# Token mixing's output sums: three float32r products per block, or one plain float32 product

## The chip, the cores and the metric

The kernel runs on one core of one Trainium2 chip. The metric is the time of one execution in device microseconds. The engines are called as the profile calls them: PE is the matrix engine (TensorE) and PEld its loads of stationary operands, DVE the vector engine, ACT the scalar engine, POOL GpSimd, SP the engine that issues most transfers. A matrix product has a stationary operand, which is loaded into the 128x128 array, and a moving operand, whose columns stream past it; the sums stand in PSUM.

## The reference

A decayed linear attention over 4 batches, 8 heads, 768 positions and head size 64, then a mixer of two parts. The attention's output is x, 4 x 768 x 512. Cut to what matters:

```
intra = (qb @ kb.T * Dmask) @ vb             # blocks of 64 positions in the reference
inter = (qb * lam_pow) @ kv_state
xt = x.transpose(0, 2, 1)                    # 4 x 512 x 768
h  = relu(xt @ w_tok1) @ w_tok2              # 768 -> 256 -> 768, over positions
u  = x + h.transpose(0, 2, 1)
h2 = relu(u @ w_ch1) @ w_ch2                 # 512 -> 1536 -> 512, over channels
out = u + h2
```

All inputs are float32 but the four weights of the mixer, which arrive as 64-bit words and are brought to float32 in the kernel. The change concerns the product with w_tok2, called w2 here.

## The kernel before, in words

**Stages.** The first stage, to about 180 us, runs the attention over 16 steps (4 batches, 4 pairs of heads each) and, mixed into it, token mixing. The second, from there to the end, is channel mixing and the output. uT[b] holds u transposed, 512 channels by 768 positions: the attention writes it (`outputs`), token mixing adds to it, channel mixing reads it.

**Token mixing.** For a batch, `token_hidden` (L442) makes the hidden layer: four calls of 128 hidden units by 256 channels, each a sum over six blocks of positions. Every operand stands in two float32r parts, high and low, and a product is three products (high by high, low by high, high by low), so a call is 18 matmuls (L459) of 256 columns. ACT then writes the rectified sum as the high part hh (L463), and DVE the low part hl (L464). `token_out` (L486) and `token_out_pair` (L469, used for the last batch) make the output: a block of 128 channels by 384 positions is a sum over two blocks of hidden units, again in three products each, so 6 matmuls of 384 columns (L496, L479). DVE adds the block to uT (L501, L484). There are 4 batches x 2 halves of positions x 4 blocks of channels = 32 blocks, so 192 matmuls.

**w2.** Its 64-bit words are loaded into the place of uT[2]. In three thirds (`w2_steps`, L432) five steps (`narrow`, L387) bring the words to float32 with scratch in the place of uT[3]: one on ACT (L392) and four on DVE (L393, L396, L399, L402). Then `split` (L383) writes the high part w2h on ACT (L384) and the low part w2l on POOL (L385).

**Plain float32 elsewhere.** The attention's own products use plain float32 operands: scores `sc` (L314: 64 rows of the array, the two heads of a pair in its upper and lower half), outputs `xT` (L333, L343: 64 columns of the array, the two heads left and right) and states `kv` (L270: 64 columns, 64 moving columns). Transposes through PE (L220, L241, L365) take a plain float32 block against an identity over the whole array.

**What sets the order.** The order on every engine is the order in which the program is written. In a step of the attention, scores of the next pair come first, then outputs, states, and between them pieces of token mixing from the list `groups` (as many per step as `take` says). Small steps for ACT, DVE and POOL, those of w2 among them, stand in a queue `waiting`, from which `later(n)` takes one to three at fixed places. Blocks of PSUM come from a ring (`sh`), so a block of output sums can wait until DVE has read an earlier one. `hidp` holds w2h, w2l, the hidden parts hh0, hl0 and h1; channel mixing uses the same places later.

Of the kernel before, what the change touches and what calls it, by code (L numbers as in the profile page):

```python
# [9 lines left out]
F32 = mybir.dt.float32  # L10
F32R = mybir.dt.float32r
AF = mybir.ActivationFunctionType
ALU = mybir.AluOpType
U32 = mybir.dt.uint32
# [8 lines left out]
def kernel(  # L23
# [23 lines left out]
    nc = tc.nc  # L47
    B, H, S, D = q.shape
    DM = H * D
    FT = w_tok1.shape[1]  # L50
    FC = w_ch1.shape[1]
    P = 128
# [3 lines left out]
    NK = FT // P  # L56
    NJ = FC // P
    SB = S // 2
# [5 lines left out]
    waiting = deque()  # L64
# [17 lines left out]
    def bank(tag, nm, n):  # L82
        if tag == "sh" and spare:
            tag = spare.pop()
        return ps.tile([P, n], F32, tag=tag, bufs={"xT": 1, "sh": 3}[tag], name=nm)

    def two_banks(nm, n):
        t = ps.tile([P, 2, 512], F32, tag="sc", bufs=2, name=nm)
        return t[:, :, 0:n]

    hidp = ctx.enter_context(tc.tile_pool(name="hidp", bufs=1, side="right"))
# [107 lines left out]
    n = 1  # L199
    while n < P:  # L200
        nc.vector.tensor_mul(
            out=lamp[:, :, n : 2 * n], in0=lamp[:, :, 0:n], in1=lamp[:, :, n - 1 : n].broadcast_to([P, NP, n])
        )
        n *= 2
    for p in range(NP):
        nc.gpsimd.tensor_copy(
            out=keep[:, p, :, 1:], in_=lamp[:, p, P - 1 : P, None].broadcast_to([P, D, NC - 2])
# [146 lines left out]
    def turn_back(i, g):  # L354
# [21 lines left out]

    w1h = tokp.tile([P, NC, FT], F32R, name="w1h")
    w1l = tokp.tile([P, NC, FT], F32R, name="w1l")
    w2h, w2l = (
        hidp.tile([P, NK, S], F32R, tag=t, name=t) for t in ("w2h", "w2l")  # L380
    )

    def split(hi, lo, src):  # L383
        nc.scalar.copy(out=hi, in_=src)  # L384
        nc.gpsimd.tensor_sub(out=lo, in0=src, in1=hi.bitcast(F32))  # L385

    def narrow(raw, a, sg):  # L387

        low, high = raw[..., 0], raw[..., 1]
        af = a.bitcast(F32)  # L390
        return [
            lambda: nc.scalar.activation(af, high.bitcast(F32), AF.Abs, scale=HIGH_SCALE),  # L392
            lambda: nc.vector.tensor_scalar(  # L393
                out=sg, in0=high, scalar1=0x80000000, scalar2=None, op0=ALU.bitwise_and
            ),
            lambda: nc.vector.scalar_tensor_tensor(  # L396
                out=sg, in0=low, scalar=29, in1=sg, op0=ALU.logical_shift_right, op1=ALU.bitwise_or
            ),
            lambda: nc.vector.tensor_scalar(  # L399
                out=af, in0=af, scalar1=HIGH_MIN * HIGH_SCALE, scalar2=HIGH_MAX * HIGH_SCALE, op0=ALU.max, op1=ALU.min  # L400
            ),
            lambda: nc.vector.scalar_tensor_tensor(  # L402
                out=a, in0=a, scalar=3, in1=sg, op0=ALU.logical_shift_left, op1=ALU.bitwise_or
            ),
        ]

    def words(b):
        return uT[b].rearrange("p t s -> p (t s)").bitcast(U32)
# [22 lines left out]

    def w2_steps(i):  # L432
        n = NK * S // 3
        tmp = words(3)[:, 2 * (i % 2) * n : 2 * (i % 2 + 1) * n]
        a, sg = (x.rearrange("p (k s) -> p k s", k=NK) for x in (tmp[:, :n], tmp[:, n:]))
        ss = slice(i * S // 3, (i + 1) * S // 3)
        raw = words(2).rearrange("p (k s two) -> p k s two", k=NK, two=2)[:, :, ss]
        return narrow(raw, a, sg) + [lambda: split(w2h[:, :, ss], w2l[:, :, ss], a.bitcast(F32))]

    hid = {}  # L440

    def token_hidden(b, half, kk):  # L442

        if half == 0 and kk == 0:
            if b % 2:
                both = hidp.tile([P, 2, NK, DM], F32R, tag="h1", name=f"h{b}")
                hid[b] = both[:, 0], both[:, 1]
            else:
                hid[b] = [hidp.tile([P, NK, DM], F32R, tag=f"{t}0", name=f"{t}{b}") for t in ("hh", "hl")]
        hh, hl = hid[b]  # L450
        xh, xl = x_of[b, half]
        cs = slice(half * DM // 2, (half + 1) * DM // 2)

        ph = bank("sh", f"ph{b}{half}{kk}", DM // 2)
        fs = slice(kk * P, (kk + 1) * P)
        i = 0
        for c in range(NC):
            for w, x in ((w1h, xh), (w1l, xh), (w1h, xl)):
                nc.tensor.matmul(  # L459
                    out=ph, lhsT=w[:, c, fs], rhs=x[:, c], start=(i == 0), stop=(i == 3 * NC - 1)  # L460
                )
                i += 1
        nc.scalar.activation(hh[:, kk, cs], ph, AF.Relu)  # L463
        nc.vector.scalar_tensor_tensor(  # L464
            out=hl[:, kk, cs], in0=ph, scalar=0.0, in1=hh[:, kk, cs].bitcast(F32), op0=ALU.max, op1=ALU.subtract
        )


    def token_out_pair(b, sh, ct):  # L469

        hh, hl = hid[b]
        pu = two_banks(f"pu{b}{ct}{sh}", SB)
        ss = slice(sh * SB, (sh + 1) * SB)
        for y in range(2):
            cs = slice((ct + y) * P, (ct + y + 1) * P)
            i = 0
            for kk in range(NK):
                for h, w in ((hh, w2h), (hl, w2h), (hh, w2l)):
                    nc.tensor.matmul(  # L479
                        out=pu[:, y], lhsT=h[:, kk, cs], rhs=w[:, kk, ss], start=(i == 0), stop=(i == 3 * NK - 1)  # L480
                    )
                    i += 1
        u = uT[b][:, ct : ct + 2, ss]
        nc.vector.tensor_add(out=u, in0=pu, in1=u)  # L484

    def token_out(b, sh, ct):  # L486

        hh, hl = hid[b]

        pu = bank("sh", f"pu{b}{ct}{sh}", SB)  # L490
        cs = slice(ct * P, (ct + 1) * P)
        ss = slice(sh * SB, (sh + 1) * SB)
        i = 0
        for kk in range(NK):
            for h, w in ((hh, w2h), (hl, w2h), (hh, w2l)):
                nc.tensor.matmul(  # L496
                    out=pu, lhsT=h[:, kk, cs], rhs=w[:, kk, ss], start=(i == 0), stop=(i == 3 * NK - 1)
                )
                i += 1
        u = uT[b][:, ct, ss]  # L500
        nc.vector.tensor_add(out=u, in0=pu, in1=u)  # L501

# [37 lines left out]
    def narrow_piece(raw, a, sg):  # L540
        return narrow(raw.rearrange("p (n two) -> p n two", two=2), a, sg)
# [91 lines left out]


    hidden = [[lambda b=b, x=x: token_hidden(b, x // NK, x % NK) for x in range(2 * NK)] for b in range(B)]
    outs = [[lambda b=b, x=x: token_out(b, x // 4, x % 4) for x in range(8)] for b in range(B)]
    groups = deque(hidden[0] + hidden[1][:NK] + outs[0] + hidden[1][NK:] + outs[1])
    for b in range(2, B):
# [6 lines left out]
    idle = [lambda: None]  # L645
# [7 lines left out]
    for i in range(-2, NI):  # L653
# [31 lines left out]
        n = early.get(i, len(work) // 4)  # L685
# [32 lines left out]
        if i == 4:  # L718
            steps = [w2_steps(n) for n in range(3)]
            waiting.extend(2 * idle + steps[0][:5] + idle + steps[0][5:] + steps[1][:2] + idle)  # L720
        if i == 5:
            waiting.extend(steps[1][2:5] + idle + steps[2][:2] + idle + steps[1][5:] + steps[2][2:] + idle)
        if i == 6:
            waiting.append(lambda: load_piece(0, 1, w3[:, 1024:2048]))
            steps = narrow_piece(w3[:, 2048:3072], w3[:, 0:512], w3[:, 512:1024])
            waiting.extend(idle + steps[:1] + 2 * idle + steps[1:2] + 2 * idle + steps[2:])
        if i == 7:
            steps = narrow_piece(w3[:, 1024:2048], w3[:, 512:1024], w3[:, 2048:2560])
# [37 lines left out]
    cs = [cp.tile([P, n * DM], U32, tag=f"cs{x}", name=f"cs{x}") for x, n in enumerate((2, 2, 1))]  # L766
# [12 lines left out]
    steps = {}  # L779
# [7 lines left out]
    for n, fs in enumerate(order):  # L787
        token_out_pair(B - 1, n // 2, 2 * (n % 2))
        for f in fs:
            f()  # L790
# [573 lines left out]
```

## Time and profile before

| | |
|---|---|
| time, median of 2 runs | 553.31 us (553.27 to 553.35) |
| the profiled execution's span | 551.6 us |
| instructions in its trace | 10805 |
| PE busy | 540.1 us of the span (98%), 4180 matmuls |
| DVE, POOL, ACT busy | 438.3, 282.0, 247.6 us |
| granted PE clock, mean | 0.999 of full speed |

The profile is of one execution; its span runs from its first to its last instruction. That execution has no separate time beside its span; the two timed runs lie 1.7 us above it, which is what lies around the span. A PE row's duration is the time of one matmul from its start to the modelled arrival of its last sum; matmuls are pipelined, so what one costs the engine is the distance from its start to the next one's start, not its duration. Busy time counts the durations where they overlap once.

### The profile page before, as it was taken

The numbers are of one execution on the slowest core, as the hardware profiler recorded it, in microseconds if no ns is written. First come the engines' busy times: TensorE is split into PE (matmuls) and PEld (weight loads), VectorE is DVE, ScalarE is ACT, GpSimd is POOL, SyncE is SP. The second block draws the span as 40 slices with busy tenths as digits, with TensorE's granted clock in tenths as the row PEclk, the third lists the DMA queues.
The fourth block names the chain that finished last, engine by engine and source line by source line (L and its number), as shares of the span: only waits on it lengthen the run. The fifth ranks groups of instructions, "written<-read, shape, count | busy, mean of one in ns | idle before, by whom it ended". The sixth has DMA issues, their size and how long they took to land.

```text
span 551.6 us, 10805 instructions
## 1 busy us (share of the span) xinstructions
PE 540.1 (98%) x4180; PEld 527.1 (96%) x4180; DVE 438.3 (79%) x657; ACT 247.6 (45%) x499; POOL 282.0 (51%) x256
## 2 busy tenths in 40 slices
PE   5999999999999999999999999999999999999997
PEld 4889998999999999999999999999999999999996
DVE  4787799687786989887878788788778878779894
ACT  3464543344253454444444443453354555445431
POOL 6667552756213564543444453354475656568450
PEclk9999999999999999999999999999999999999999
DMA  9999999999103523351615300024766132220186
GB/s 185 252 209 193 222 172 182 197 197 157 32 2 114 198 91 118 124 197 43 252 70 203 121 1 1 0 30 65 169 115 198 58 116 58 95 97 2 22 156 130
DMA packets 175683, 66.77 MB, mean 121 GB/s; under 512 B 163600, under 2 KB 165904, under 8 KB 175632
## 3 DMA queue, kind: packets, MB, share of 16 engines
q1 hardware_dynamic: 170400, 64.90, 49.2%
q10 hardware_dynamic: 5232, 1.18, 1.0%
q8 instruction: 33, 0.54, 0.4%
q14 instruction: 18, 0.15, 0.1%
HBM read 49.29 MB, written 16.78 MB: 120 GB/s over the span
## 4 chain that ended last, share of the span: by engine, by line
PE 92%; DMA 3%; DVE 2%; SPq 1%; issue 0%; ACT 0%; ACTq 0%; DVEq 0%
PE po L1043 22%; PE pa L817 13%; PE pc L817 9%; PE pb L817 7%; PE pa L1017 7%; PE ph L459 6%; PE pc L1017 5%; DMA qn<-in_q_dram 3%; PE sc L314 3%; PE pu L496 3%; PE xT L333 3%; PE pd L817 3%; PE xT L343 2%; PE xp L365 2%; PE pu L479 2%; PE kv L270 1%
## 5 line engine op out<-in xcount | busy, mean ns | idle before, releaser
L1056 DVE TENSOR_TENSOR uT<-po,uT 128x768 f32<-128x768 f32 x57 | 54.2, 952 | 16.7 <-PE po L1043 16.4
L832 ACT ACTIVATE c<-c 128x384 f32<-128x384 f32 x42 | 22.1, 526 | 59.2 <-DVE c L877 33.5
L291 POOL COPY stb<-sv 64x320 f32<-64x320 f32 x32 | 26.9, 840 | 38.8 <-DVE sv L278 37.9
L1023 DVE TENSOR_TENSOR uT<-pa,uT 128x768 f32<-128x768 f32 x36 | 34.3, 953 | 9.4 <-PE pa L1017 8.6
L350 ACT COPY uT<-xT 128x384 f32<-128x384 f32 x32 | 15.3, 479 | 46.8 <-PE xT L343 46.7
L834 POOL TENSOR_TENSOR h22l<-c,h22h 128x384 fp32r<-128x384 f32 x14 | 14.4, 1032 | 41.5 <-ACT h22h L833 41.5
L333 PE MATMUL xT<-a,vn 128*64 128x128 f32 x384 | 35.7, 277 | 0.0
L1023 DVE TENSOR_TENSOR uT<-pc,uT 128x768 f32<-128x768 f32 x27 | 25.8, 954 | 11.1 <-PE pc L1017 11.1
L298 DVE TENSOR_TENSOR a<-sc,mask 128x768 f32<-128x768 f32 x32 | 29.1, 947 | 4.6 <-PE sc L314 4.5
L343 PE MATMUL xT<-qs,stb 128*64 128x128 f32 x320 | 31.3, 273 | 0.0
L385 POOL TENSOR_TENSOR c1l<-cs,c1h 128x512 fp32r<-128x512 f32 x15 | 19.3, 1297 | 22.9 <-ACT c1h L384 22.9
L1043 PE MATMUL po<-h12h,c 128*128 128x384 f32 x112 | 28.7, 337 | 0.0
L1043 PE MATMUL po<-h11h,c 128*128 128x384 f32 x112 | 28.6, 336 | 0.0
L1043 PE MATMUL po<-h22h,c 128*128 128x384 f32 x112 | 28.6, 336 | 0.0
L1043 PE MATMUL po<-h21h,c 128*128 128x384 f32 x112 | 28.6, 336 | 0.0
L459 PE MATMUL ph<-xhi,w1h 128*128 128x256 f32 x96 | 28.1, 293 | 0.1
L459 PE MATMUL ph<-xhi,w1l 128*128 128x256 f32 x96 | 27.1, 282 | 0.0
L459 PE MATMUL ph<-xlo,w1h 128*128 128x256 f32 x96 | 27.1, 282 | 0.0
L314 PE MATMUL sc<-qT,kT 64*128 64x128 f32 x384 | 25.8, 281 | 0.3 <-ACT qT L242 0.2
L314 PEld LDWEIGHTS sc<-qT,kT 64*128 64x128 f32 x384 | 22.8, 188 | 3.5 <-issue 2.0
L374 DVE TENSOR_TENSOR xlo<-xp,xhi 128x384 fp32r<-128x384 f32 x32 | 17.7, 552 | 10.3 <-ACT xhi L373 10.0
L257 POOL TENSOR_TENSOR qs<-qT,lamp 128x640 f32<-128x640 f32 x16 | 25.5, 1594 | 0.2
(397 smaller groups left out, 1945.0 us busy)
## 6 DMA issues: line engine op xcount, KB each, us to landing
raw<-in_moe_w_ch_dram SPq DMA_DIRECT2D x20, 512.0 KB, 3.8
vn<-in_v_dram SPq DMA_DIRECT2D x16, 384.0 KB, 5.3
kn<-in_k_dram SPq DMA_DIRECT2D x30, 192.0 KB, 5.2
out_dram<-y SPq DMA_DIRECT2D x104, 48.0 KB, 1.9
qn<-in_q_dram SPq DMA_DIRECT2D x44, 96.0 KB, 3.9
kr<-in_k_dram SPq DMA_DIRECT2D x32, 96.0 KB, 2.7
dc1h<-c1h SPq DMA_DIRECT2D x4, 768.0 KB, 5.4
dc1l<-c1l SPq DMA_DIRECT2D x4, 768.0 KB, 6.7
```

The lines of the kernel that those rows point to most:

```text
L257: nc.gpsimd.tensor_mul(out=qss[i], in0=qTs[i][:, P:].rearrange("p (c i) -> p c i", i=P), in1=lamp[:, p, None, :].broadcast_to([P, NC - 1, P]),
L291: nc.gpsimd.tensor_copy(out=st[r, :, h, :], in_=sv[r].rearrange("p (e c) -> p c e", c=NC - 1))
L298: nc.vector.tensor_mul(out=a, in0=pair.rearrange("p h (c i) -> p h c i", i=P), in1=mask[:, 2 * p : 2 * p + 2, None, :].broadcast_to([P, 2, ...
L314: nc.tensor.matmul(out=sc[h][:, c * P : (c + 1) * P], lhsT=kTs[i][r, cs], rhs=qTs[i][r, cs], start=True, stop=True,)
L333: nc.tensor.matmul(out=xT[h * D : (h + 1) * D, cs], lhsT=vns[i][:, h, c, :], rhs=weights_of[i, g, h][:, cg, :], start=(cg == 0), stop=False,)
L343: nc.tensor.matmul(out=xT[h * D : (h + 1) * D, cs], lhsT=st[:, c - 1, h, :], rhs=qss[i][:, c - 1, :], start=False, stop=(cg == 2),)
L459: nc.tensor.matmul(out=ph, lhsT=w[:, c, fs], rhs=x[:, c], start=(i == 0), stop=(i == 3 * NC - 1))
L817: nc.tensor.matmul(out=to, lhsT=w[:, t], rhs=x[:, t], start=(start and i == 0), stop=(i == 5), skip_group_check=not start,)
L1017: nc.tensor.matmul(out=pair[x][:, t], lhsT=w[:, t], rhs=h, start=(start and i == 0), stop=(i == 2), skip_group_check=not start,)
L1023: nc.vector.tensor_add(out=ub, in0=pair[x], in1=ub)
L1043: nc.tensor.matmul(out=to, lhsT=w[:, jj, t * P : (t + 1) * P], rhs=h, start=(i == 0), stop=(i == 3 * JG - 1))
L1056: nc.vector.tensor_add(out=ub, in0=po, in1=ub)
```

## The change

Token mixing's output sums use plain float32 operands. The hidden layer is written once by ACT, without a low part; w2 is one float32 tile, which the narrowing steps write in place, without a split. Per block of 128 channels by 384 positions there are two products in the program's text in place of six. The hidden sums over w1 and all of channel mixing stay in three products.

```
--- before.py
+++ after.py
@@ -376,9 +376,7 @@
 
     w1h = tokp.tile([P, NC, FT], F32R, name="w1h")
     w1l = tokp.tile([P, NC, FT], F32R, name="w1l")
-    w2h, w2l = (
-        hidp.tile([P, NK, S], F32R, tag=t, name=t) for t in ("w2h", "w2l")
-    )
+    w2 = hidp.tile([P, NK, S], F32, tag="w2h", name="w2")
 
     def split(hi, lo, src):
         nc.scalar.copy(out=hi, in_=src)
@@ -431,23 +429,19 @@
 
     def w2_steps(i):
         n = NK * S // 3
-        tmp = words(3)[:, 2 * (i % 2) * n : 2 * (i % 2 + 1) * n]
-        a, sg = (x.rearrange("p (k s) -> p k s", k=NK) for x in (tmp[:, :n], tmp[:, n:]))
+        sg = words(3)[:, (i % 2) * n : (i % 2 + 1) * n].rearrange("p (k s) -> p k s", k=NK)
         ss = slice(i * S // 3, (i + 1) * S // 3)
+        a = w2.bitcast(U32)[:, :, ss]
         raw = words(2).rearrange("p (k s two) -> p k s two", k=NK, two=2)[:, :, ss]
-        return narrow(raw, a, sg) + [lambda: split(w2h[:, :, ss], w2l[:, :, ss], a.bitcast(F32))]
+        return narrow(raw, a, sg)
 
     hid = {}
 
     def token_hidden(b, half, kk):
 
         if half == 0 and kk == 0:
-            if b % 2:
-                both = hidp.tile([P, 2, NK, DM], F32R, tag="h1", name=f"h{b}")
-                hid[b] = both[:, 0], both[:, 1]
-            else:
-                hid[b] = [hidp.tile([P, NK, DM], F32R, tag=f"{t}0", name=f"{t}{b}") for t in ("hh", "hl")]
-        hh, hl = hid[b]
+            hid[b] = hidp.tile([P, NK, DM], F32, tag="h1" if b % 2 else "hh0", name=f"h{b}")
+        h = hid[b]
         xh, xl = x_of[b, half]
         cs = slice(half * DM // 2, (half + 1) * DM // 2)
 
@@ -460,43 +454,34 @@
                     out=ph, lhsT=w[:, c, fs], rhs=x[:, c], start=(i == 0), stop=(i == 3 * NC - 1)
                 )
                 i += 1
-        nc.scalar.activation(hh[:, kk, cs], ph, AF.Relu)
-        nc.vector.scalar_tensor_tensor(
-            out=hl[:, kk, cs], in0=ph, scalar=0.0, in1=hh[:, kk, cs].bitcast(F32), op0=ALU.max, op1=ALU.subtract
-        )
-
+        nc.scalar.activation(h[:, kk, cs], ph, AF.Relu)
+
+
+    def token_products(to, b, sh, ct):
+
+        for kk in range(NK):
+            nc.tensor.matmul(
+                out=to,
+                lhsT=hid[b][:, kk, ct * P : (ct + 1) * P],
+                rhs=w2[:, kk, sh * SB : (sh + 1) * SB],
+                start=(kk == 0),
+                stop=(kk == NK - 1),
+            )
 
     def token_out_pair(b, sh, ct):
 
-        hh, hl = hid[b]
         pu = two_banks(f"pu{b}{ct}{sh}", SB)
         ss = slice(sh * SB, (sh + 1) * SB)
         for y in range(2):
-            cs = slice((ct + y) * P, (ct + y + 1) * P)
-            i = 0
-            for kk in range(NK):
-                for h, w in ((hh, w2h), (hl, w2h), (hh, w2l)):
-                    nc.tensor.matmul(
-                        out=pu[:, y], lhsT=h[:, kk, cs], rhs=w[:, kk, ss], start=(i == 0), stop=(i == 3 * NK - 1)
-                    )
-                    i += 1
+            token_products(pu[:, y], b, sh, ct + y)
         u = uT[b][:, ct : ct + 2, ss]
         nc.vector.tensor_add(out=u, in0=pu, in1=u)
 
     def token_out(b, sh, ct):
 
-        hh, hl = hid[b]
-
         pu = bank("sh", f"pu{b}{ct}{sh}", SB)
-        cs = slice(ct * P, (ct + 1) * P)
         ss = slice(sh * SB, (sh + 1) * SB)
-        i = 0
-        for kk in range(NK):
-            for h, w in ((hh, w2h), (hl, w2h), (hh, w2l)):
-                nc.tensor.matmul(
-                    out=pu, lhsT=h[:, kk, cs], rhs=w[:, kk, ss], start=(i == 0), stop=(i == 3 * NK - 1)
-                )
-                i += 1
+        token_products(pu, b, sh, ct)
         u = uT[b][:, ct, ss]
         nc.vector.tensor_add(out=u, in0=pu, in1=u)
 
@@ -719,7 +704,7 @@
             steps = [w2_steps(n) for n in range(3)]
             waiting.extend(2 * idle + steps[0][:5] + idle + steps[0][5:] + steps[1][:2] + idle)
         if i == 5:
-            waiting.extend(steps[1][2:5] + idle + steps[2][:2] + idle + steps[1][5:] + steps[2][2:] + idle)
+            waiting.extend(steps[1][2:5] + idle + steps[2][:2] + idle + steps[2][2:] + idle)
         if i == 6:
             waiting.append(lambda: load_piece(0, 1, w3[:, 1024:2048]))
             steps = narrow_piece(w3[:, 2048:3072], w3[:, 0:512], w3[:, 512:1024])
```

On PE, the first blocks of output sums of batch 0 (`pu`) behind the attention's outputs (`xT`), between transposes (`xp`). Before:

```order
L343 MATMUL xT_1199<-qs_1022,stb_119 64x128 x2
L496 MATMUL pu_1218<-w2h,hh_768 128x384
L496 MATMUL pu_1218<-w2h,hl_769 128x384
L496 MATMUL pu_1218<-w2l,hh_768 128x384
L496 MATMUL pu_1218<-w2h,hh_768 128x384
L496 MATMUL pu_1218<-w2h,hl_769 128x384
L496 MATMUL pu_1218<-w2l,hh_768 128x384
L365 MATMUL xp_1227<-ident,uT_61 128x128 x3
```

With the change:

```order
L343 MATMUL xT_1187<-qs_1015,stb_119 64x128 x2
L463 MATMUL pu_1204<-w_137,h_767 128x384 x2
L365 MATMUL xp_1209<-ident,uT_61 128x128 x3
L463 MATMUL pu_1221<-w_137,h_767 128x384 x2
L463 MATMUL pu_1228<-w_137,h_767 128x384 x2
```

The six rows of a block become two, at the same place among the others; `w_137` is the one tile of w2. These rows are the program's matmuls: the listing does not say how many the chip executes for one.

On DVE, the first third of w2 (`uT_62` the words, `uT_63` scratch) between the low parts `xlo` of x. Before:

```order
L393 TENSOR_SCALAR uT_63<-uT_62 128x512
L464 SCALAR_TENSOR_TENSOR hl_769<-ph_929,hh_768 128x256
L396 SCALAR_TENSOR_TENSOR uT_63<-uT_62,uT_63 128x512
L399 TENSOR_SCALAR uT_63<-uT_63 128x512
L402 SCALAR_TENSOR_TENSOR uT_63<-uT_63 128x512
L374 TENSOR_TENSOR xlo_813<-xp_953,xhi_812 128x3x128
L464 SCALAR_TENSOR_TENSOR hl_769<-ph_959,hh_768 128x256
L298 TENSOR_TENSOR a_1011<-sc_1004,mask 128x768
```

With the change:

```order
L391 TENSOR_SCALAR uT_63<-uT_62 128x512
L394 SCALAR_TENSOR_TENSOR uT_63<-uT_62,uT_63 128x512
L397 TENSOR_SCALAR w_137<-w_137 128x2x256
L400 SCALAR_TENSOR_TENSOR w_137<-w_137,uT_63 128x2x256
L374 TENSOR_TENSOR xlo_809<-xp_948,xhi_808 128x3x128
L391 TENSOR_SCALAR uT_63<-uT_62 128x512
L298 TENSOR_TENSOR a_1004<-sc_997,mask 128x768
```

The low parts `hl` are gone, the last narrowing steps write w2 itself, and the next third's first step has moved up before the masked scores `a`, since the queue holds fewer steps. On POOL the three rows `w2l` are gone, on ACT the three copies `w2h`; SP's order of transfers is unchanged.

## Rows read from the trace of the kernel before

**Rows 1.** The page, busy time by engine and granted clock over 40 slices.

```profile
PE 540.1 (98%) x4180; PEld 527.1 (96%) x4180; DVE 438.3 (79%) x657; ACT 247.6 (45%) x499; POOL 282.0 (51%) x256
...
PEclk9999999999999999999999999999999999999999
```

**Rows 2.** Busy time by stretch: PE, PEld, DVE, ACT, POOL, clock, DMA.

```profile
8.00:75.00 67.00, 65.00 (x912) 59.54 (x914) 52.10 (x78) 34.85 (x78) 40.78 (x38) 1.00 1.07 212
75.00:180.00 105.00, 104.13 (x1160) 98.78 (x1157) 85.32 (x130) 42.96 (x86) 48.58 (x42) 1.00 0.66 130
180.00:552.00 372.00, 367.82 (x2102) 366.49 (x2100) 298.30 (x440) 167.05 (x331) 188.49 (x166) 1.00 0.36 101
```

**Rows 3.** Waits of PE's weight loads, 75 to 180 us: waited for, us, times, longest.

```profile
PEld sc L314 <- issue: 1.0, 4, 0.2
PEld pu L496 <- ACT kd L250: 0.9, 1, 0.9
PEld pu L496 <- issue: 0.7, 4, 0.2
...
PEld ph L459 <- DVE uT L501: 0.3, 1, 0.3
```

**Rows 4.** Busy time by stretch of the output sums' tile pu alone: PE, PEld, DVE.

```profile
75.00:180.00 105.00, 37.59 (x192) 32.56 (x192) 16.98 (x28) 1.00 0.66 130
```

**Rows 5.** Timeline, output sums in three parts: start us, us, engine, line, tiles.

```profile
79.09 0.33 PE L496 MATMUL pu<-w2h,hl 128*128 128x384 f32 x1
79.09 0.19 PEld L496 LDWEIGHTS pu<-w2l,hh 128*128 128x128 f32 x1
79.27 0.33 PE L496 MATMUL pu<-w2l,hh 128*128 128x384 f32 x1
79.27 0.19 PEld L496 LDWEIGHTS pu<-w2h,hh 128*128 128x128 f32 x1
...
81.86 0.34 PE L496 MATMUL pu<-w2l,hh 128*128 128x384 f32 x1
```

**Rows 6.** Timeline of all engines, the longest wait of the output sums.

```profile
81.64 0.96 DVE L234 STREAM_TRANSPOSE kT<-kr 128x768 f32<-128x768 f32 x1
...
82.04 0.49 PE L365 MATMUL xp<-ident,uT 128*128 128x128 f32 x3
...
82.53 0.52 DVE L501 TENSOR_TENSOR uT<-pu,uT 128x384 f32<-128x384 f32 x1
...
83.19 0.41 PE L496 MATMUL pu<-w2h,hh 128*128 128x384 f32 x1 [0.66 <-DVE uT L501]
```

**Rows 7.** Timeline of PE, plain float32 products on half the array, merged by line.

```profile
107.51 0.50 PE L314 MATMUL sc<-qT,kT 64*128 64x128 f32 x6
107.94 0.66 PE L333 MATMUL xT<-a,vn 128*64 128x128 f32 x8
108.43 0.39 PE L343 MATMUL xT<-qs,stb 128*64 128x128 f32 x4
108.64 0.39 PE L333 MATMUL xT<-a,vn 128*64 128x128 f32 x4
108.86 0.39 PE L343 MATMUL xT<-qs,stb 128*64 128x128 f32 x4
109.08 0.75 PE L270 MATMUL kv<-vn,kd 128*64 128x64 f32 x20
109.66 0.39 PE L333 MATMUL xT<-a,vn 128*64 128x128 f32 x4
```

**Rows 8.** Timeline of PE, scores up to 106.65 us and up to 106.75 us.

```profile
106.40 0.49 PE L314 MATMUL sc<-qT,kT 64*128 64x128 f32 x4
...
106.40 0.60 PE L314 MATMUL sc<-qT,kT 64*128 64x128 f32 x6
```

**Rows 9.** Timeline of PE, hidden sums and transposes, both on the whole array.

```profile
102.28 0.28 PE L459 MATMUL ph<-xhi,w1l 128*128 128x256 f32 x1
102.40 0.28 PE L459 MATMUL ph<-xlo,w1h 128*128 128x256 f32 x1
102.52 0.49 PE L365 MATMUL xp<-ident,uT 128*128 128x128 f32 x3
```

**Rows 10.** Groups by line: tiles, shapes, count, busy us, mean ns, idle before.

```profile
L459 PE MATMUL ph<-xhi,w1h 128*128 128x256 f32 x96 | 28.1, 293 | 0.1
...
L314 PE MATMUL sc<-qT,kT 64*128 64x128 f32 x384 | 25.8, 281 | 0.3 <-ACT qT L242 0.2
...
L365 PE MATMUL xp<-ident,uT 128*128 128x128 f32 x96 | 15.8, 279 | 0.2
```

**Rows 11.** Removed work: DVE's low parts (line 464), POOL's w2l (its tile).

```profile
0.00:180.00 180.00, 6.77 (x16) 1.00 0.82 162
...
L385 POOL TENSOR_TENSOR w2l<-uT,w2h x3: 1279/1295/1538, 64.1 to 80.4; 128x512 fp32r<-128x512 f32 x3
```

## The prediction, made before the changed kernel ran

> **What bounds the kernel now.** The busy shares come first: PE is busy 98% of the span and its clock is granted in full throughout [rows 1]. That alone says little, since PE's rows are pipelined, so the shares by stretch follow: from 75 to 180 us PE is busy 104.13 of 105.00 us, while DVE has 85.32, POOL 48.58 and ACT 42.96; after 180 us it is 367.82 of 372 [rows 2]. All 192 matmuls of token mixing's output sums lie in the first of these stretches [rows 4]. The waits of PE's weight loads there are small: the four around this work come to 2.9 us [rows 3]. So PE sets the end: a column streamed more or less on PE is paid or saved in full, and work taken off the other engines is worth at most what PE waits for them. What a matmul costs PE is then read from the distance between starts in the timeline, not from its duration.
>
> **What PE no longer does.** From the matmul at 79.09 us to the one at 81.86 us there are 16 distances, 2.77 us, so 0.173 us each [rows 5]; 384 columns at the granted 2.4 GHz are 0.160, and 0.013 lies on top. The 192 matmuls cost 192 x 0.173 = 33.2 us. The Trainium skill ("TensorE: Matmul & The Clock Gate", section "Back-to-back issue gap") gives columns / 2.4 GHz plus 2.5 ns, which is 0.1625 us here; this trace differs by 0.011 us in each matmul. By the page's formula alone the removed work would be 31.2 us and 128 added matmuls with twice 384 columns 41.3 us, an estimate of +10.1 us in place of the +8.8 below; the measured distance decides.
>
> **What PE does in its place.** 64 plain float32 products of the whole array with 384 columns (32 blocks, two products each). First, how many matmuls that is. The program has 16 pairs x 2 groups x 3 blocks x 2 heads = 192 score products, and the trace shows 384 matmuls for them; the hidden sums have 96 products of each kind and show 96 [rows 10]. A plain float32 product is two matmuls, so 128 come.
>
> Second, what one costs. No row shows a plain float32 product on the whole array, so I bound it. Attention's products are on half the array, two heads side by side. Four such matmuls with 128 columns (two heads, two matmuls each) take 0.21 to 0.22 us from start to start, twenty with 64 columns 0.58 us [rows 7]. Per pair of matmuls this is 0.108 and 0.058: 64 columns more cost 0.050 us, 0.78 ns a column, about two cycles at 2.4 GHz. Scores add 0.11 us per pair [rows 8]. I read it as two halves working at the same time, each matmul streaming its columns twice. The transposes support that on the whole array, alone: three take 0.49 us and one lasts 0.279 [rows 9, 10], so their distance is (0.49 - 0.279) / 2 = 0.106 us or slightly more, 128 columns twice. With 384 columns a matmul therefore streams 2 x 384 / 2.4 = 320 ns. The overhead per matmul is 2 ns or so in the plain float32 rows [rows 7, 9] and 13 ns for float32r on the whole array (0.173 here; 0.12 for 256 columns, where streaming is 0.107) [rows 5, 9]. The operation is like the first in its format and like the second in its weights, so I take the middle, 0.328 us, with the ends 0.322 and 0.333. 128 x 0.328 = 42.0 us, between 41.2 and 42.6.
>
> PE's net: 42.0 - 33.2 = **+8.8 us** (+8.0 to +9.4). Four times the columns of one pass against three times: the new form is longer by a third of a product, less the third matmul's overhead.
>
> **What the other engines no longer do.** DVE loses 16 low parts of the hidden layer, 6.77 us in all, POOL three low parts of w2 at about 1.3 us each [rows 11], ACT three copies. All lie beside PE, whose 104.13 of 105.00 us [rows 2] is the cover, so by themselves they give nothing. Where they could matter is PE's waits. The longest stands at 82.3 us: PE has issued transposes at 82.04, the next block of output sums starts at 83.19 and waited for DVE to empty a block, and that DVE addition, at 82.53, stood behind a transpose of loaded rows that runs from 81.64 [rows 6]. Four output blocks precede it in this step of the attention, each now 2 x 2 x 0.328 - 6 x 0.173 = 0.27 us longer, so PE comes there about 1.1 us later and this wait is covered: **-0.8 us**. What would be late next is PE itself. Ends: no gain (0), if DVE slips with PE; -1.2 us, if the 0.3 us before the hidden sums goes too, with the 0.9 [rows 3].
>
> **What moves.** The narrowing of w2's next third comes earlier on DVE, ahead of a masked score that PE's attention outputs wait for. One such step is 0.6 us (estimated from POOL's and DVE's rows of similar width, such as the 0.52 us addition of 384 elements in [rows 6]), with slack of about 20 us on DVE in the stretch [rows 2]; I take 0 and keep +0.6 as an end. The first output sums now wait for the narrowing itself in place of the copy and low part behind it, a shorter chain: 0. Channel mixing's loads into the place of the old low parts may start sooner; there PE is busy 367.82 of 372 us [rows 2]: 0. The hidden layer's write by ACT stays as it is.
>
> **Sum.** +8.8 - 0.8 = +8.0 us, from +8.0 - 1.2 = +6.8 to +9.4 + 0.6 = +10.0. Against the profiled execution: 551.6 + 8.0 = 559.6 us of span; 1.7 us lie around it, and span plus this is the median of the two timed runs, 553.3. So the time is 553.3 + 8.0 = **561.3 us**, 1.4% more, between 560.1 and 563.3.
>
> **Rival 1, faster: the whole array streams each plain matmul once.** The half-array rows can be read otherwise: the two halves may take turns, each matmul streaming its 128 columns once in 0.054 us [rows 7, 8]. Then 128 matmuls cost as float32r ones do, 128 x 0.173 = 22.1 us, and PE saves 11.1 us; with 0.2 us of wait gone the time is 542.0 us. The point from which this decides is a distance of 0.26 us per matmul (33.2 / 128), below which the change gains. Against it: a transpose, alone on the whole array, has the distance of two passes [rows 9], and a score matmul with 128 columns is modelled as long (281 ns) as one of the hidden sums with 256 (293) [rows 10]. The Trainium skill ("FP8 and Floating Point Precision", section "TensorE Precision Notes") states that true float32 takes four passes through the array, which is the other reading, two matmuls of two passes; the transposes' distance here agrees with it. Chance 0.05.
>
> **Rival 2, slower by more: weight loads come into the open.** If the load of a plain float32 block into the whole array can't run beside the matmul before it, each of 128 matmuls pays for it. The price is that of a change of form: the last three pairs of scores take 107.51 to 107.94, 0.43 us, where three pairs take 0.33, so 0.10 us [rows 7, 8]. For all 128 that is +12.8 us, 574.1; for the first of each product +6.4, 567.7. Against it: in the same tile before the change, each load starts with the matmul ahead of it (79.09 and 79.09, 79.27 and 79.27), and matmuls still follow at 0.173 [rows 5]. The Trainium skill ("TensorE: Matmul & The Clock Gate", section "The mechanism") says that a weight load overlaps matmuls in flight only where the row groups differ, and by that no whole-array load would be hidden; rows 5 do not agree. Chance 0.10.
>
> **Rival 3: the other engines' relief is worth more.** If all 2.9 us of the waits listed [rows 3] went, the time would be 553.3 + 8.8 - 2.9 = 559.2 us, and with the low end of PE's net (+8.0) 558.4. Against it: 1.7 us of them are PE's own issue, which the removed work doesn't touch. Chance 0.03.
>
> **How the numbers follow.** The forecast has 0.82. About 2%, 11 us, is what a measurement of this kernel can tell from no change, so the limits are 542.2 and 564.4. Forecast and rival 3 lie within: 0.85. Rival 1 is faster: 0.05. Rival 2 is slower: 0.10. The range takes in the forecast's ends and rival 3, 558.4 to 564.4 with 1 us above 563.3 for an overhead larger than 13 ns, and leaves out rivals 1 and 2, 0.15.
>
> **What would show it.** The output sums' tile should have 128 matmuls in place of 192, at distances of 0.322 to 0.333 us within a block; 0.17 would be rival 1, 0.38 or more, with loads that no longer start with the matmul ahead, rival 2. The wait of 0.66 us for DVE at the fifth block should be gone. No low parts of the hidden layer or of w2 should be left on DVE and POOL. From the first rows of channel mixing on, all should be the same, only about 8 us later. I would be wrong by the sum if PE's waits grew between 75 and 180 us, most likely at masked scores on DVE.

## The result and the profile after

The changed kernel takes 560.4 us (560.36 to 560.44), against 553.31 before: a ratio of 1.0124, 95% interval 1.0105 to 1.0143. That is 7.1 us more, where 8.0 was forecast; the span went from 551.6 to 558.6 us. The first two rows are the page's busy shares and clock, the next two the busy time by stretch (PE, PEld, DVE, ACT, POOL, clock, DMA), which answer to [rows 1, 2].

```profile
PE 547.4 (98%) x4116; PEld 517.9 (93%) x4116; DVE 434.3 (78%) x641; ACT 246.1 (44%) x496; POOL 277.7 (50%) x253
...
PEclk9999999999999999999999999999999999999999
```

```profile
75.00:188.00 113.00, 112.59 (x1100) 90.19 (x1097) 83.44 (x119) 42.69 (x86) 44.95 (x39) 1.00 0.61 121
188.00:560.00 372.00, 366.87 (x2097) 365.82 (x2096) 295.48 (x439) 166.94 (x331) 188.07 (x165) 1.00 0.36 101
```

PE is still the bound, at the full clock, and fuller than before in the stretch of the change: 112.59 of 113.00 us. The other engines have less to do there. Behind this stretch channel mixing starts later and is otherwise as before, within 0.2 us.

Next, the output sums' tile alone: its matmuls and loads (least, median and longest duration in ns; first and last start), then the timeline of PE around the fourth and fifth block, to be held against [rows 5, 6].

```profile
L463 PEld LDWEIGHTS pu<-w,h x128: 186/190/192, 77.4 to 183.5; 128*128 128x128 f32 x128
L463 PE MATMUL pu<-w,h x128: 483/486/591, 77.4 to 183.9; 128*128 128x384 f32 x128
```

```profile
79.15 4.04 PE L463 MATMUL pu<-w,h 128*128 128x384 f32 x12
83.03 0.49 PE L365 MATMUL xp<-ident,uT 128*128 128x128 f32 x3
83.83 1.56 PE L463 MATMUL pu<-w,h 128*128 128x384 f32 x4 [0.31 <-DVE uT L486]
```

There are 128 matmuls for 64 products, two each. Twelve in a row last 4.04 us, so their distance is (4.04 - 0.486) / 11 = 0.323 us; the 111 distances inside blocks have a median of 0.323. 128 x 0.323 = 41.3 us against 33.2 of before: +8.1 us, or +8.0 with the distances taken more finely (128 x 0.3225 - 192 x 0.1735). The wait for DVE at the fifth block is 0.31 us, where it was 0.66. DVE's own rows there, for the same stretch, show why it did not go:

```profile
81.67 0.96 DVE L234 STREAM_TRANSPOSE kT<-kr 128x768 f32<-128x768 f32 x1
82.55 0.75 DVE L391 TENSOR_SCALAR uT<-uT 128x512 uint32<-128x512 uint32 x1
83.23 1.01 DVE L486 TENSOR_TENSOR uT<-pu,uT 128x384 f32<-128x384 f32 x2
```

The transpose ends at the time of before, but a narrowing step of 0.75 us now stands ahead of the two additions. Before, the first addition stood there [rows 6] and a narrowing step only behind it. The queue of small steps has become shorter, and a step has slid into this place.

The other wait that shrank is in the next step of the attention, where hidden sums wait for DVE to empty a block [rows 3]. PE before, then after:

```profile
92.65 0.49 PE L365 MATMUL xp<-ident,uT 128*128 128x128 f32 x3
93.25 0.38 PE L459 MATMUL ph<-xhi,w1h 128*128 128x256 f32 x1
```

```profile
94.29 0.49 PE L365 MATMUL xp<-ident,uT 128*128 128x128 f32 x3
94.54 0.37 PE L453 MATMUL ph<-xhi,w1h 128*128 128x256 f32 x1
```

From the transposes to the hidden sums it takes 0.25 us in place of 0.60. So +8.0 on PE, -0.35 and -0.35 in two waits and -0.2 behind 188 us make 7.1 us, where the span has 7.0. In a step without waits the account closes to 20 ns: the step from 106.40 to 117.15 us before has five blocks and took 1.23 us longer, and 5 x (4 x 0.3225 - 6 x 0.1735) is 1.245.

### The profile page after: what moved, and what is told of

Its sections match the earlier page's. It is cut to its first block, busy times and chain, and to the rows that moved or that the text cites. A ratio compares the mean times of both kernels' runs of the same rounds, so it can differ in the third digit from the quotient of the medians.

```text
span 558.6 us, 10651 instructions
## 1 busy us (share of the span) xinstructions
PE 547.4 (98%) x4116; PEld 517.9 (93%) x4116; DVE 434.3 (78%) x641; ACT 246.1 (44%) x496; POOL 277.7 (50%) x253
## 4 chain that ended last, share of the span: by engine, by line
PE 95%; DMA 2%; DVE 1%; SPq 1%; issue 0%; ACT 0%; ACTq 0%; DVEq 0%
PE po L1028 21%; PE pa L802 12%; PE pc L802 9%; PE pb L802 7%; PE pa L1002 7%; PE pu L463 7%; PE ph L453 6%; PE pc L1002 5%; PE sc L314 4%; PE xT L333 4%; PE xT L343 3%; PE pd L802 3%; PE xp L365 2%; PE kv L270 1%; DMA qn<-in_q_dram 1%; DMA kn<-in_k_dram 1%
## 5 line engine op out<-in xcount | busy, mean ns | idle before, releaser
L463 PE MATMUL pu<-w,h 128*128 128x384 f32 x128 | 44.7, 491 | 0.3 <-DVE uT L486 0.3
L350 ACT COPY uT<-xT 128x384 f32<-128x384 f32 x32 | 15.3, 478 | 51.2 <-PE xT L343 51.1
L463 PEld LDWEIGHTS pu<-w,h 128*128 128x128 f32 x128 | 23.0, 190 | 13.9 <-issue 0.7
L383 POOL TENSOR_TENSOR c1l<-cs,c1h 128x512 fp32r<-128x512 f32 x15 | 19.3, 1296 | 23.2 <-ACT c1h L382 23.2
```

Source lines behind the costliest of these rows:

```text
L463: nc.tensor.matmul(out=to, lhsT=hid[b][:, kk, ct * P : (ct + 1) * P], rhs=w2[:, kk, sh * SB : (sh + 1) * SB], start=(kk == 0), stop=(kk == ...
```

## The experiments

Two theories stood at the start. **A**: PE's columns are paid in full, and the 1 us given back is PE coming later to blocks that DVE must empty. **B**: it is the relief of DVE, ACT and POOL that gave it back. The rivals on what one plain matmul costs were tested beside them. All times are medians; before took 553.4 us on the first chip and 553.3 to 553.5 on the others.

**The change again, on the same chip as the next three.**

> The changed kernel once more, beside the others on one chip. Both theories: 560.4 us, ratio 1.0128 (553.31 + 7.1); its span was 7.0 us longer than that of before.

It took 560.5 us, ratio 1.013 [1.0115, 1.0146].

**Plain products, all low parts still made.** An edit of the kernel before:

```
-                for h, w in ((hh, w2h), (hl, w2h), (hh, w2l)):
+                for h, w in ((hh, w2h),):
...
-  lhsT=h[:, kk, cs], rhs=w[:, kk, ss]
+  lhsT=h[:, kk, cs].bitcast(F32), rhs=w[:, kk, ss].bitcast(F32)
```

> The kernel before with one plain float32 product per block of hidden units in place of three, on the high parts alone: the low parts of hidden layer and w2 are still made by DVE and POOL, but no product reads them (the output lacks them). On PE it is the changed kernel, on DVE, ACT and POOL the one before. 64 products cost +8.1 us on PE (128 x 0.3225 - 192 x 0.1733); about 1.0 us of that came back in waits. Theory A (the waits went because PE now comes later to the same blocks): they go here too, 560.4 us, within 0.4. Theory B (they went because DVE, ACT and POOL have less to do): they stay here, 561.4 us.

It took 560.49 us, ratio 1.0127 [1.0113, 1.0141]. The stretch of token mixing (PE, PEld, DVE, ACT, POOL, clock, DMA):

```profile
74.00:184.50 110.50, 110.40 (x1111) 88.25 (x1111) 85.72 (x129) 42.55 (x85) 49.13 (x41) 1.00 0.63 122
```

DVE and POOL do their old work, 85.72 and 49.13 us, and PE has no gap: 110.40 of 110.50. In this stretch the trace has no wait of PE for DVE at all, not even the 0.31 us; the queue of small steps is as long here as before. Theory A's mechanism holds, and B falls: the lateness alone removes the waits.

That the time is the change's, 560.5 us, is luck. Its four runs are 559.79, 559.96, 561.01 and 561.08 us, and the median lies between two pairs. The profiled one is the last. It waited longer for loads of k and q than the change did, and reached the step of the first output sums 1.2 us later. PE's waits for loads here, then in the change:

```profile
PE kt L220 <- DMA kn<-in_k_dram: 5.2, 2, 4.7
PE qt L241 <- DMA qn<-in_q_dram: 2.7, 4, 1.0
```

```profile
PE kt L220 <- DMA kn<-in_k_dram: 5.7, 3, 5.2
PE qt L241 <- DMA qn<-in_q_dram: 0.9, 1, 0.9
```

That step, from scores to scores, is shorter here than in the change. Before, the change, and this run:

```profile
72.76:84.40 11.64, 10.98 (x125) 10.17 (x124) 10.60 (x17) 4.82 (x10) 8.04 (x6) 1.00 0.95 182
```

```profile
72.76:85.32 12.56, 12.25 (x116) 8.69 (x116) 10.20 (x17) 3.78 (x8) 3.45 (x3) 1.00 0.98 183
```

```profile
73.96:85.95 11.99, 11.99 (x116) 8.66 (x115) 10.72 (x17) 4.95 (x10) 7.93 (x6) 1.00 1.00 192
```

Five blocks cost 1.245 us more on PE. With the old queue 0.35 of it is left, so the lateness gave back 0.9; in the change 0.92 is left, so 0.57 was lost again, where the narrowing step has slid ahead of the additions. The two runs at 559.8 and 560.0 us, 0.5 to 0.6 below the change, fit this. Dropping the low parts did not help the change: with the shorter queue that came of it, it cost about 0.6 us.

**Three products, no low parts made.** The relief without the longer products:

```
-   return narrow(raw, a, sg) + [lambda: split(w2h[:, :, ss], w2l[:, :, ss], a.bitcast(F32))]
+   return narrow(raw, a, sg) + [lambda: nc.scalar.copy(out=w2h[:, :, ss], in_=a.bitcast(F32))]
...
-   nc.vector.scalar_tensor_tensor(out=hl[:, kk, cs], ...)
...
-   for h, w in ((hh, w2h), (hl, w2h), (hh, w2l)):
+   for h, w in ((hh, w2h), (hh, w2h), (hh, w2h)):
```

> The kernel before, still with six float32r matmuls per block, but no low parts are made: the high parts take their place in all three products (the output lacks the low parts). DVE loses 6.8 us, POOL 4.1 us, PE nothing. Theory A (relief of the other engines is worth nothing while PE is the bound): 553.3 us, 553.0 to 553.4. Theory B (relief is what gave the 1.0 us): 552.3 us.

It took 553.61 us, ratio 1.0004 [0.9995, 1.0012]. Its waits of PE between 75 and 180 us (waited for, us, times, longest):

```profile
PE pu L493 <- DVE uT L498: 0.4, 1, 0.4
PE ph L459 <- DVE uT L498: 0.2, 1, 0.2
```

Both waits are still there. The first is shorter (0.4 us where it was 0.66), the second is not: PE itself waits 0.2 us there. With PE as the bound, 6.8 us of DVE and 4.1 us of POOL are worth nothing that can be measured. The queue keeps its length here, since a copy stands in place of each split, and no narrowing step slides ahead of the additions.

**Each plain product cut into four of 96 columns, then into two of 192.** The same columns, more matmuls and loads:

```
+        n = SB // 4        # SB // 2 in the second
+        for x in range(4): # range(2)
             for kk in range(NK):
...
-                out=to, ... rhs=w2[:, kk, sh * SB : (sh + 1) * SB],
+                out=to[:, x * n : (x + 1) * n], ... rhs=w2[:, kk, sh * SB + x * n : sh * SB + (x + 1) * n],
```

> The changed kernel with each plain product cut into four of 96 columns: the same columns stream, in 512 matmuls in place of 128, each with its own weight load. If a matmul streams its columns twice and adds 2.5 ns: 512 x (0.080 + 0.0025) = 42.2 us against 41.3, +0.9 us, 561.3. If the overhead is that of float32r (13 ns): 512 x 0.093 = 47.6 us, 566.7. If the weight load of a whole plain block (0.11 us, the distance of scores with as many weight columns) becomes the bound: 512 x 0.11 = 56.3 us, 575.

> The changed kernel with each plain product cut into two of 192 columns: 256 matmuls, each 0.160 + 0.0025 us of streaming if its weight load (0.112 us at 96 columns) hides beside it: 41.6 us against 41.3, 560.8 us. If weight load and streaming add up in part, 0.01 us a matmul is +2.6 us, 563.

They took 575.76 us (ratio 1.0398 [1.0381, 1.0415]) and 561.13 us (1.0143 [1.0126, 1.016]). The timeline of PE, quarters and then halves, and between them the duration of the quarters' matmuls:

```profile
80.21 3.04 PE L465 MATMUL pu<-w,h 128*128 128x96 f32 x26
```

```profile
L465 PE MATMUL pu<-w,h x512: 247/275/350, 78.0 to 199.5; 128*128 128x96 f32 x171
```

```profile
79.42 3.90 PE L465 MATMUL pu<-w,h 128*128 128x192 f32 x23
```

Quarters follow each other at (3.04 - 0.275) / 25 = 0.111 us (median 0.112), although two passes of 96 columns take 0.080. Something else sets this distance. Scores, with as many weight columns, follow at 0.11 too [rows 8], but they stream 128 columns, whose two passes are 0.107, so they cannot tell a load from the streaming. The quarters' own loads, and the matmuls beside them, say more:

```profile
80.10 0.75 PEld L465 LDWEIGHTS pu<-w,h 128*128 128x128 f32 x6
80.21 0.69 PE L465 MATMUL pu<-w,h 128*128 128x96 f32 x5
```

The loads follow each other at (0.75 - 0.192) / 5 = 0.112 us and last 0.19, so each starts before the one ahead has ended, and the matmuls keep their pace. 512 x 0.112 = 57.3 us, 16 more than 41.3; the time rose by 15.3. Halves follow at 0.163 us (the median of their distances): two passes of 192 columns, 0.160, and 0.0025. The runs fit a plain matmul that costs the longer of its two passes and its load of about 0.11 us, hidden as long as the passes are longer. That it is the load, and not another floor of 0.11 us, is argued: no run left the loads out. Rival 2's mechanism may thus exist, but not at 384 columns.

**The hidden sums as plain products too.** Another size, another place:

```
-   for w, x in ((w1h, xh), (w1l, xh), (w1h, xl)):
-       nc.tensor.matmul(out=ph, lhsT=w[:, c, fs], rhs=x[:, c], ...)
+   nc.tensor.matmul(out=ph, lhsT=w1h[:, c, fs].bitcast(F32), rhs=xh[:, c].bitcast(F32), ...)
```

> The changed kernel with the hidden sums over w1 also as one plain float32 product, on the high parts alone (low parts of x and w1 are still made, no product reads them; the output lacks them). 288 float32r matmuls of 256 columns at 0.1195 us (34.4 us) become 192 plain ones. Two passes and 2.5 ns: 192 x 0.2158 = 41.4 us, +7.0 us, 567.4, up to 0.5 less where waits are covered. If a plain matmul carried a fixed cost in place of a second pass (0.3225 = 0.160 + 0.1625): 192 x 0.269 = 51.7 us, +17.3 us, 577.7.

It took 567.58 us, ratio 1.0253 [1.0238, 1.0268]. Its hidden sums by line (count, busy us, mean ns) and in the timeline:

```profile
L452 PE MATMUL ph<-xhi,w1h 128*128 128x256 f32 x192 | 43.9, 380 | 0.0
```

```profile
48.14 5.13 PE L452 MATMUL ph<-xhi,w1h 128*128 128x256 f32 x23
```

(5.13 - 0.380) / 22 = 0.216 us for 256 columns. From 192 to 256 and 384 columns the distances are 0.163, 0.216 and 0.323: 0.83 ns a column, two passes at 2.4 GHz, with some 2.5 ns on top. A fixed cost in place of the second pass is excluded.

**The other direction: two products in place of three.** If PE is paid in full on the way up, is it on the way down?

```
-   for h, w in ((hh, w2h), (hl, w2h), (hh, w2l)):
+   for h, w in ((hh, w2h), (hl, w2h)):
```

> The kernel before with the third product (high part of the hidden layer by low part of w2) left out: 128 float32r matmuls of 384 columns in place of 192. If PE's columns are paid in full, 64 x 0.1733 = 11.1 us go: 542.2 us, or up to 1.5 us more, since PE comes earlier to blocks that DVE must empty (theory A makes these waits grow). If another engine becomes the bound: 546 us or more.

It took 549.62 us, ratio 0.9935 [0.9921, 0.9948]: 3.8 us of 11.1. Only the last alternative, another engine as the bound and 546 us or more, takes that in, and it gave no size. The waits of PE for DVE grew, as A has it, but 7 us were lost, not 1.5. Its waits of PE in token mixing, and one step of the attention (from scores to scores) before and here:

```profile
PE pu L496 <- DVE xlo L374: 1.1, 2, 0.8
PE pu L496 <- DVE uT L501: 1.1, 2, 0.9
PE ph L459 <- DVE uT L501: 0.7, 1, 0.7
```

```profile
84.40:95.60 11.20, 11.09 (x132) 10.35 (x131) 10.84 (x18) 3.41 (x7) 3.54 (x3) 1.00 0.97 190
```

```profile
85.20:96.40 11.20, 10.27 (x127) 9.26 (x126) 11.20 (x19) 3.46 (x7) 3.53 (x3) 1.00 1.03 192
```

Three blocks lie in this step, so PE has 1.04 us less to do, and the step is as long as before: DVE is busy 10.84 of its 11.20 us before and 11.20 of 11.20 with two products. The share of DVE over the whole stage [rows 2] had hidden a step in which it is full.

Another part of the loss lies behind token mixing. At the start of channel mixing PE adds to a block that DVE must read first (`pb`), and waits 1.7 us for it, with DVE busy throughout. The kernel before has no such wait:

```profile
PE pb L817 <- DVE u L859: 1.7, 1, 1.7
```

```profile
175.20:177.10 1.90, 0.28 (x2) 0.00 (x0) 1.90 (x4) 0.79 (x2) 0.72 (x1) 1.00 0.64 246
```

**Less work for DVE, then fewer loads.** Two runs with two products each:

```
-   for h, w in ((hh, w2h), (hl, w2h)):        # first: no hl made, DVE relieved
+   for h, w in ((hh, w2h), (hh, w2l)):
...
-            kr = kp.tile([P, S], F32, tag="kr", bufs=2, name=f"kr{i}")   # second, on top
-            load_dims(kr, k, b, p)
-            krs[i] = kr
+            krs[i] = kn.rearrange("p c h d -> p (c h d)")
```

> Two float32r products per block as before this run, but high part of the hidden layer by high and by low part of w2, so that DVE makes no low part of the hidden layer: 6.8 us less on DVE, the same matmuls on PE (the output lacks the hidden layer's low part). Theory A (with two products DVE holds PE up): 543 to 547 us in place of 549.6. Rival (the lost gain has another cause, such as loads or ACT): 549 to 550.

> The run with two products and no low part of the hidden layer (548.2 us), but from step 8 on the second load of k, by head dimension (four transfers of 96 KB a step, 32 in all), is left out; DVE's transpose reads the first load of k in its place (the output is then wrong from there on). PE, DVE, ACT and POOL do the same work. In that run PE's stage from 72.8 us on was 6.9 us shorter than before the change where 11.1 us of matmuls are gone. Theory C (once PE has less to do, the queue of loads and what DVE does behind them set the pace of the attention's steps): 2 to 4 us more come free, 544 to 546.5. Rival (DVE's own work sets it, the loads only happen to end there): 548, within 0.7.

They took 548.19 us (ratio 0.9904 [0.989, 0.9919]) and 548.2 us (0.9907 [0.9889, 0.9925]). The first gave 1.4 us more. That is neither the range of A (543 to 547) nor that of its rival (549 to 550): DVE's low part was a part of the loss, and not most of it. Its chain of waits from 84 to 140 us pointed at loads, hence the second run. The lines are the chain's shares by engine and line, of the changed kernel and of two products without that low part.

```profile
by line: PE pu L463 28.9%; PE ph L453 23.4%; PE sc L314 13.7%; PE xT L333 13.1%; PE xT L343 9.7%; PE xp L365 6.4%; PE kv L270 5.2%
```

```profile
by line: PE ph L459 15.4%; SPq L115 14.0%; PE sc L314 8.2%; PE xT L333 7.8%; DMA uT<-in_moe_w_ch_dram 6.1%; SPq L137 6.0%; PE xT L343 5.8%; DMA kr<-in_k_dram 5.1%; DVE uT L498 5.0%; DVE qT L230 3.2%; PE kv L270 3.1%; DVE kT L234 3.1%; PE xp
```

In the changed kernel the chain never leaves PE; with two products it runs through the queue of loads (SPq) and the transfers. Theory C, that loads set the pace, was not borne out: 32 transfers less changed nothing. The loads that remain were not tested. The same step of the attention in that run:

```profile
83.60:94.80 11.20, 10.27 (x126) 9.24 (x124) 11.11 (x19) 3.46 (x7) 3.53 (x3) 1.00 0.39 71
```

The DMA share fell to 0.39, and the step is still 11.20 us long, with DVE busy 11.11 of it. So it is DVE's own work in its own order that holds this step, as far as the rows show; a chain that follows the last wait backward can end in loads whose absence changes nothing. The wait at the start of channel mixing is 1.4 us in the run without the low part. The rest of the lost gain was not tried further: the step at 104.7 us takes 10.9 us with 9.0 of DVE, and PE's waits there are for low parts of x and for additions behind transposes.

**The kernel before with fewer loads.** The same edit on three products:

> The kernel before, with the second load of k left out from step 8 on in the same way (the output is wrong from there on). If PE is the bound with three parts, as the prediction has it: 553.3 us, at most 1.0 less (its three waits for DVE). If loads held PE up before the change too: 550 to 551.

It took 553.36 us, ratio 0.9999 [0.999, 1.0009]. These loads did not hold PE before either.

**One product.**

```
-   for h, w in ((hh, w2h), (hl, w2h), (hh, w2l)):   # and no hl, no w2l made
+   for h, w in ((hh, w2h),):
```

> The kernel before with one float32r product of the high parts per block of hidden units, and no low parts made (the output lacks them). 64 matmuls of 384 columns in place of 192: on PE alone 22.2 us less, 531.2. With three products less one, half of the 11.1 us came back in waits of PE for DVE; DVE has 6.8 us less here. Theory A (what PE saves is worth only as far as DVE keeps up): 533 to 542, likeliest 538. Rival (PE alone counts): 531 to 532.

It took 552.15 us, ratio 0.9967 [0.9949, 0.9984], its runs from 548.7 to 553.25. Both expectations missed by 10 us and more: 128 matmuls less than before are worth 1.2 us. The busy time in two of its steps, in four short stretches of the first, and the hidden sums there:

```profile
83.20:97.40 14.20, 12.18 (x119) 11.07 (x118) 11.54 (x20) 3.46 (x7) 3.51 (x3) 0.76 1.04 184
...
118.30:129.30 11.00, 11.00 (x133) 10.55 (x132) 8.22 (x11) 5.60 (x12) 8.02 (x6) 0.89 1.02 190
```

```profile
89.00:91.00 2.00, 2.00 (x19) 1.55 (x15) 2.00 (x4) 0.96 (x2) 1.67 (x3) 1.00 1.27 267
91.00:93.00 2.00, 0.63 (x4) 0.31 (x3) 2.00 (x4) 1.54 (x3) 1.84 (x1) 1.00 1.37 202
93.00:95.00 2.00, 1.35 (x6) 1.36 (x7) 2.00 (x6) 0.48 (x2) 0.00 (x0) 0.62 1.10 147
95.00:97.00 2.00, 2.00 (x12) 2.00 (x11) 1.06 (x2) 0.00 (x0) 0.00 (x0) 0.53 0.67 104
```

```profile
95.09 0.41 PE L459 MATMUL ph<-xhi,w1h 128*128 128x256 f32 x1
95.31 0.41 PE L459 MATMUL ph<-xhi,w1l 128*128 128x256 f32 x1
```

From 91 to 93 us PE is busy 0.63 of 2.00 us, waiting for DVE, which has no gap. In the two stretches behind that the granted clock is 0.62 and 0.53, about its lower level of 1.2 GHz, and hidden sums follow at 0.21 to 0.22 us where they took 0.12 [rows 9]. The step takes 14.2 us against 11.2. Taking more work off PE made it wait, and behind the waits its clock was lower, so that the rest of the work became dearer. The step at 118.3 us shows that price alone: it has no block of output sums, PE is busy all of it, and it takes 11.0 us where it took 9.8.

The ten runs go with the clock: 548.7 and 549.6 us at a mean of 0.993, 550.5 and 552.1 at 0.991, 552.1 to 553.3 at 0.987 and 0.988. But the clock is the smaller part. A mean of 0.988 over 550.6 us is at most 6.6 us of full clock, an estimate, and 21 of 22.2 us were lost. More of it is waiting: the time in which PE is not busy grew from 11.5 us before (551.6 - 540.1) to 23.2 (550.6 - 527.4), 3.2 us of it at the start of channel mixing, where two products lost 1.7.

## Why the prediction was right

**The bound.** PE set the end before and does so after. Relief of the other engines alone gave nothing (553.61 against 553.39 us), and neither did leaving out 32 of the loads (553.36).

**The price of a plain product.** The step that carried the forecast was to read two passes per matmul out of products on half the array and transposes on the whole. It held: 0.322 to 0.323 us, 0.216 at 256 columns, 0.163 at 192. Of the ends 0.322 and 0.333 the lower was right; the overhead of float32r (13 ns) does not belong to whole-array weights but to that format, since plain products on the whole array have 2.5. The middle was 0.7 us too dear. The Trainium skill ("FP8 and Floating Point Precision", section "TensorE Precision Notes") has four passes for true float32; two matmuls of two passes agree with it. By the formula of the Trainium skill ("TensorE: Matmul & The Clock Gate", section "Back-to-back issue gap"), with twice 384 columns put in, the added matmuls cost 41.3 us, an estimate that the trace bears out; the removed ones would have been 31.2 and were 33.2, so that its sum of +10.1 was off by what it does not have, the longer distance of float32r.

**The waits.** Forecast -0.8 us from one wait; measured -0.35 there and -0.35 at another, which had stood only in the low end. The wait at the fifth block was to vanish and halved. What was missed is an effect of the shorter queue: I had looked for the narrowing step that moves up ahead of a masked score, and it moved ahead of two additions. With the queue's length kept (plain products with all low parts made) the wait is gone, as forecast, and gave back 0.9 us. The step that moved was put at 0, with +0.6 kept as an end; it cost 0.57. That the waits together, -0.7, came near the forecast's -0.8 is luck: of the 0.9 at the first wait the moved step took back 0.57, and the second wait, which the middle of the forecast did not have, gave 0.35.

**The rivals.** Rival 1 (one pass) fell with the distances. Rival 2 (open loads) fell at 384 columns: loads of 0.19 us lie beside passes of 0.32. The Trainium skill ("TensorE: Matmul & The Clock Gate", section "The mechanism") has a weight load overlap matmuls in flight only where the row groups differ, though it also has loads into a background weight buffer pulled ahead; by the first rule alone no whole-array load would be hidden, and these rows do not agree with that. At 96 columns something of the size of a load is the bound, so the rival may have its right place there. Rival 3 fell: the relief by itself is worth nothing here.

## What to carry to other kernels

Cost a plain float32 product as two matmuls of two passes each; against three float32r products it loses about a quarter of their time at 384 columns (0.645 against 0.520 us) where PE is the bound, and the work that it saves elsewhere pays nothing there. Work that is saved off the bound can still move other steps: here a shorter queue put one in PE's way, for 0.57 us. Work added to the bound is paid nearly in full, but work taken off it, as far as its loss was traced here, is paid only down to the next engine's fullest step, which can lie behind the stage: look at the busy shares step by step, not over the stage, before promising a gain. Dropping one of three products gained 3.8 us of 11.1, and dropping two gained 1.2 of 22.2, mostly for waits and in part for a clock that was lower behind them; the fastest kernel here had two products and no low part of the hidden layer (548.2 us, 0.99 of before), whose output lacks that part.

## What the runs showed of the hardware

A plain float32 matmul of 96 columns with its own load of 128 columns followed another at 0.111 us, where its two passes are 0.080. A float32r matmul followed 13 ns later than its columns take (0.173 at 384 columns), a plain one 2.5 ns later than its two passes (0.163 at 192, 0.216 at 256, 0.323 at 384). In the run with one product a stretch of 2 us in which PE was busy 0.63 us was followed by a granted clock of 0.62 and 0.53.
